# A one-token attention layer with a gated second branch: four 32 KB buffers become a ring of three

## The chip, the cores and the metric

The kernel runs on one core of one Trainium2 chip. The metric is the device time of one execution in microseconds. Before the change the median of five runs is 81.89 us (81.75 to 81.96).

## The reference

One token `x` (1 x 512) goes through two branches, and a scalar gate mixes them:

```python
g = sigmoid((x * gate_w).sum(-1))
q = (x @ wq).reshape(32 heads, 128)
k, v = k_cache[:, :, Sk - 4096:], v_cache[:, :, Sk - 4096:]   # 8 kv heads, 4 q heads on each
p = softmax(q @ k.T * 128 ** -0.5)
a = (p @ v).reshape(1, 4096) @ wo                             # wq: 512 x 4096, wo: 4096 x 512
b = (sigmoid(x @ w_gate) * (x @ w_up)) @ w_down               # 512 x 1792, 512 x 1792, 1792 x 512
out = g * a + (1 - g) * b
```

All tensors are bf16. `wq` and `wo` hold 4 MB each, the used part of `k_cache` and of `v_cache` 8 MB each, the three matrices of the second branch 1.75 MB each. All of it is read once.

## The kernel before

The kernel is written with tile pools: a tile is asked for with a tag, the tiles of a tag rotate through the `bufs` buffers of the pool, and a tile that takes over a buffer waits until the readers of the tile before it are done. The waits are put in by the framework from the order of the program.

Large loads are all issued from SP, whose queue is in order, so the program's order of loads is the order in which they are issued: `wq` (L76), K 0-3 and K 4-7 (L79, called from L85), `w_gate` (L89), `w_up` (L91), V 0-3 and V 4-5 (L79), V 6, the first half of `w_down` (L105), V 7, the second half of `w_down` (L107), and `wo` in six pieces of 8, 8, 8, 5, 2 and 1 rows of each partition (L112). A digit behind K or V is the number of a kv head. A load that waits for a buffer holds up every load behind it. ACT issues the two 1 KB rows `x` and `gate_w` at the start and half of the result at the end; SP issues the other half (L295).

Three pools hold these loads, given in bytes of one partition. `big` has one buffer of 32 KB: `wq_sb` first, then `wo_sb`. `blk` has two buffers of 32 KB: K 0-3 and K 4-7, then V 0-3 in the buffer of K 0-3 and V 4-7 in that of K 4-7. `w14` has three of 14 KB, one for each matrix of the second branch, so nothing waits there.

The work of the engines, in order of the program:

- `x` is turned into a column on PE (L133, `xT`), and DVE and ACT make the gate from it (L141 to L150).
- q (L155 to L164): for each of four blocks of 1024 columns, eight matmuls on PE with `xT` spread over all columns (L160, four slices `c` of `wq`, two halves each, `c` in the outer loop), then a copy by ACT (L162) and a transpose by DVE (L163). DVE then places q in `qbig` (L172).
- scores (L178 to L188): for each kv head DVE transposes K (L180, `kT`, from `kn`) and PE multiplies (L185, eight matmuls, all heads in `S_ps`). `kT` shares a ring of four 8 KB buffers with `q_sb` and `qtT`.
- softmax and the second branch up to `hT` (L191 to L240) on DVE, ACT and PE.
- V (L257 to L279): two batches of four kv heads on PE (L267), with part of the product with `w_down` between them (L248, called from L263 and L274).
- the end: the rows of `wo` are added to the accumulator `a_ps` in the order of the pieces (L248, called from L292); two copies (L294 on DVE, L296 on ACT) and two stores of 512 bytes end the kernel.

Of the kernel before, what the change touches and what calls it, by code (L numbers as in the profile page):

```python
# [12 lines left out]
BF16 = mybir.dt.bfloat16  # L13
# [4 lines left out]
def kernel(  # L18
# [16 lines left out]
    P = 128  # L35
# [8 lines left out]
    KB = W // P  # L44
# [11 lines left out]
    NJ_A = NJ // 2  # L56

    const = ctx.enter_context(tc.tile_pool(name="const", bufs=1))
    big = ctx.enter_context(tc.tile_pool(name="big", bufs=1))
    blk = ctx.enter_context(tc.tile_pool(name="blk", bufs=2))  # L60
    w14 = ctx.enter_context(tc.tile_pool(name="w14", bufs=3))
    ktp = ctx.enter_context(tc.tile_pool(name="ktp", bufs=4))
    work = ctx.enter_context(tc.tile_pool(name="work", bufs=1))
# [9 lines left out]
    dq = nc.sync  # L73
    wq_sb = big.tile([P, DC, HQ * DH], BF16, name="wq_sb", tag="big")
    wq_v = A_wq.rearrange("(p c) n -> p c n", c=DC)
    dq.dma_start(wq_sb[:], wq_v)  # L76

    def load_blocks(t, cache, g0, n, at=0):
        dq.dma_start(t[:, at:at + n, :, :],  # L79
                     cache[0, g0:g0 + n, SBASE:SBASE + W, :].rearrange("g (p kb) d -> p g kb d", kb=KB))  # L80

    kn = []
    for i in range(2):
        t = blk.tile([P, 4, KB, P], BF16, name="kn", tag="blk")
        load_blocks(t, A_k_cache, 4 * i, 4)  # L85
        kn += [t[:, j] for j in range(4)]

# [7 lines left out]

    vv = []
    for i in range(2):
        t = blk.tile([P, 4, KB, P], BF16, name="vv", tag="blk")
        vv += [t[:, j] for j in range(4)]
        if i == 0:  # L100
            load_blocks(t, A_v_cache, 0, 4)
        else:
            load_blocks(t, A_v_cache, 4, 2)
            load_blocks(t, A_v_cache, 6, 1, at=2)
            dq.dma_start(wd_sb[:, 0:NJ_A, :], wd_v[:, 0:NJ_A, :])  # L105
            load_blocks(t, A_v_cache, 7, 1, at=3)
            dq.dma_start(wd_sb[:, NJ_A:NJ, :], wd_v[:, NJ_A:NJ, :])  # L107
# [220 lines left out]
```

## Time and profile before

| what | value |
|---|---|
| median of five runs | 81.89 us (81.75 to 81.96) |
| the profiled execution, its own time | 81.75 us |
| its span, from the first to the last instruction | 80.0 us |
| busy: PE, DVE, ACT, POOL | 48.6, 35.1, 8.8, 5.0 us |
| bytes read, mean rate over the span | 30.67 MB, 384 GB/s |
| packet time of SP's queue, share of 16 DMA engines over the span | 92.4% |
| mean granted TensorE clock | 0.893 |

Busy time is the time in which an engine executes; a line of the chain of waits says what the work that ended last was waiting for, step by step from the end. A wait on SP (`SPq`) is a load that could not be issued. "DMA share" in a table by stage is packet time divided by 16 engines and the length of the stage; packets of one engine overlap a little, so it can be a few hundredths over 1. The span leaves out 1.75 us of the profiled execution's time, which lie around it.

### The profile page before, as it was taken

To read this page: it belongs to the slowest core of one execution; us is meant where nothing else is said; L and a number is where in the kernel's file an instruction comes from. 1 tells how busy PE (TensorE), PEld (TensorE's weight loads), DVE (VectorE), ACT (ScalarE), POOL (GpSimd) and SP (SyncE) were. 2 spreads that over 40 slices of the span, in tenths; PEclk is the share of its full clock that TensorE was granted. 3 is DMA by queue.
4 is the path that set the end of the run, shared out by engine and by line. 5 is a ranking of instruction groups with operands and counts; after the bars stand their busy time and mean duration, and the time that the engine had idled before them with its cause. 6 is when DMAs were issued, how large, how long until landed. Compare 5 with 4: busy or idle time off the path is not lost.

```text
span 80.0 us, 774 instructions
## 1 busy us (share of the span) xinstructions
PE 48.6 (61%) x313; PEld 22.8 (29%) x313; DVE 35.1 (44%) x43; ACT 8.8 (11%) x13; POOL 5.0 (6%) x10
## 2 busy tenths in 40 slices
PE   0010114999800099999998980006999699679560
PEld 0000111344200033344443430003333445356330
DVE  0000820014359999999995449998000000020020
ACT  2400000055630000000000036000000200200010
POOL 7970000000000000000000000000000000000000
PEclk9999999999999655699999999555558999999999
DMA  5879979999999999999999999999999999999500
GB/s 148 311 328 525 443 344 381 422 430 430 422 422 430 410 430 423 425 459 430 409 411 418 418 414 426 422 418 430 412 413 429 429 420 422 426 402 403 214 10 1
DMA packets 3738, 30.71 MB, mean 384 GB/s; under 512 B 276, under 2 KB 408, under 8 KB 920
## 3 DMA queue, kind: packets, MB, share of 16 engines
q1 hardware_dynamic: 3730, 30.67, 92.4%
q8 instruction: 2, 0.03, 0.2%
q10 hardware_dynamic: 6, 0.00, 0.0%
HBM read 30.67 MB, written 0.00 MB: 384 GB/s over the span
## 4 chain that ended last, share of the span: by engine, by line
DMA 56%; DVE 23%; PE 12%; issue 3%; ACT 1%; DVEq 0%
DMA wo_sb<-in_A_wo_dram 23%; DVE kT L180 20%; DMA vv<-in_A_v_cache_dram 18%; DMA wq_sb<-in_A_wq_dram 15%; PE q_ps L160 11%; DVE qbig L172 2%; PE a_ps L248 2%; ACT q_sb L162 1%; DVE qtT L163 1%; DVE res L294 1%; DVEq L180 0%; DVEq L172 0%
## 5 line engine op out<-in xcount | busy, mean ns | idle before, releaser
L185 PE MATMUL S_ps<-kT,qbig 128*128 128x512 bf16 x64 | 17.0, 428 | 6.4 <-DVE kT L180 6.4
L180 DVE STREAM_TRANSPOSE kT<-kn 128x2048 f32<-128x2048 f32 x8 | 17.7, 2274 | 0.0
L267 PE MATMUL pv_ps<-vv,eT 128*16 128x512 bf16 (+1 forms) x64 | 12.0, 464 | 0.0
L185 PEld LDWEIGHTS <-qbig 128*128 128x128 bf16 x64 | 6.8, 106 | 16.5 <-issue 6.6
L160 PE MATMUL q_ps<-wq_sb,xT 128*128 128x512 bf16 x32 | 8.6, 436 | 2.8 <-DMA wq_sb<-in_A_wq_dram 2.8
L163 DVE STREAM_TRANSPOSE qtT<-q_sb 128x512 f32<-128x512 f32 x4 | 2.8, 711 | 9.6 <-ACT q_sb L162 9.6
L279 DVE TENSOR_TENSOR oT<-o_ps,rb 128x16 bf16<-128x16 f32 x2 | 0.4, 176 | 14.5 <-PE o_ps L277 14.5
L267 PEld LDWEIGHTS <-eT 128*16 128x16 bf16 (+1 forms) x64 | 4.5, 103 | 6.4 <-issue 3.6
L160 PEld LDWEIGHTS <-xT 128*128 128x128 bf16 x32 | 3.5, 110 | 7.5 <-issue 4.9
L162 ACT CAST q_sb<-q_ps 128x1024 bf16<-128x1024 f32 x4 | 4.0, 1012 | 8.2 <-PE q_ps L160 8.2
L248 PE MATMUL a_ps<-wo_sb,oY 128*1 128x256 bf16 x64 | 4.2, 272 | 1.1 <-DMA wo_sb<-in_A_wo_dram 1.1
L237 PE MATMUL rb_ps<-lsel,ones_f 128*128 128x32 f32 x2 | 0.6, 397 | 6.9 <-DVE lsel L235 6.9
L141 DVE TENSOR_TENSOR gpr<-xr 1x512 f32<-1x512 bf16 x1 | 0.7, 680 | 8.2 <-DMA xr<-in_gate_w_dram 8.2
L126 POOL MEMSET qbig<- 128x4160 bf16 x1 | 3.6, 3566 | 0.0
L248 PEld LDWEIGHTS <-oY 128*1 128x1 bf16 x64 | 2.8, 83 | 2.4 <-issue 1.5
L133 PE MATMUL xt_ps<-ident,xr 1*128 1x1 bf16 x4 | 0.3, 165 | 5.2 <-POOL ident L118 5.2
L272 ACT COPY pv_sb<-pv_ps 128x512 f32<-128x512 f32 x2 | 1.2, 586 | 19.1 <-PE pv_ps L267 19.1
L221 ACT ACTIVATE sge<-gu_ps 128x448 f32<-128x448 f32 x1 | 0.5, 544 | 24.6 <-PE gu_ps L215 24.6
L144 PE MATMUL z_ps<-gsum,ones_f 1*128 1x1 f32 x2 | 0.6, 358 | 4.2 <-DVE gsum L142 4.2
L224 DVE RECIPROCAL sg<-sge 128x448 f32<-128x448 f32 x1 | 3.0, 2953 | 0.0
L277 PE MATMUL o_ps<-identf,pv_sb 128*128 128x16 f32 x16 | 2.1, 265 | 1.4 <-ACT pv_sb L272 1.4
L294 DVE CAST res<-a_ps 1x256 bf16<-1x256 f32 x1 | 0.4, 411 | 5.8 <-PE a_ps L248 5.8
(49 smaller groups left out, 28.2 us busy)
## 6 DMA issues: line engine op xcount, KB each, us to landing
kn<-in_A_k_cache_dram SPq DMA_DIRECT2D x2, 4096.0 KB
wq_sb<-in_A_wq_dram SPq DMA_DIRECT2D x1, 4096.0 KB, 12.3
vv<-in_A_v_cache_dram SPq DMA_DIRECT2D x1, 4096.0 KB, 18.2
wo_sb<-in_A_wo_dram SPq DMA_DIRECT2D x3, 1024.0 KB, 22.7
vv<-in_A_v_cache_dram SPq DMA_DIRECT2D x1, 2048.0 KB
vv<-in_A_v_cache_dram SPq DMA_DIRECT2D x2, 1024.0 KB, 16.5
wg_sb<-in_B_w_gate_dram SPq DMA_DIRECT2D x1, 1792.0 KB, 35.0
wu_sb<-in_B_w_up_dram SPq DMA_DIRECT2D x1, 1792.0 KB, 32.5
```

The costliest lines, as they stand in the source:

```text
L126: nc.gpsimd.memset(qbig[:], 0.0)
L160: nc.tensor.matmul(q_ps[:, hb, :], lhsT=xT[:, c:c + 1].to_broadcast([P, P]), rhs=wq_sb[:, c, n0:n0 + 512], start=(c == 0), stop=(c == DC - 1))
L162: nc.scalar.copy(q_sb[:, k * 1024:(k + 1) * 1024], q_ps[:].rearrange("p a b -> p (a b)"))
L163: nc.vector.transpose(qtT[:].bitcast(F32)[:, k * 512:(k + 1) * 512], q_sb[:].bitcast(F32)[:, k * 512:(k + 1) * 512])
L172: nc.vector.tensor_copy(q_dst[rows, :, 32 * qd:32 * qd + REP, :, t], q_src[rows, :, :, :, 0, t])
L180: nc.vector.transpose(kT[:].bitcast(F32), kn[g].rearrange("p k d -> p (k d)").bitcast(F32))
L185: nc.tensor.matmul(S_ps[:, hb, :], lhsT=q_st[:, g, dhi, :, t], rhs=k_v[:, hb * 16:(hb + 1) * 16, dhi, :, t], start=(g == 0 and dhi == 0 an ...
L224: nc.vector.reciprocal(sg[:], sge[:])
L248: nc.tensor.matmul(a_ps[32 * i:32 * i + 1, i, 0:HN], lhsT=lhsT, rhs=rhs[:, i * HN:(i + 1) * HN], start=start, stop=stop)
L267: nc.tensor.matmul(pv_ps[32 * gq:32 * gq + mm, :, :], lhsT=eT[:, g, 4 * m:4 * m + wj, :].rearrange("p k h -> p (k h)"), rhs=vv[g][:, 4 * m ...
L277: nc.tensor.matmul(o_ps[:], lhsT=pv_sb[:, j, :], rhs=sel_v[:, j, :, :], start=(j == 0), stop=(j == 3))
L294: nc.vector.tensor_copy(res[0:1, :], a_ps[0:1, 0, 0:HN])
```

## The change

The pool `blk` goes away. `wq`, K 0-3, K 4-7, V 0-3, V 4-7 and `wo` now share one ring of three 32 KB buffers under one tag. They take the buffers in this order, so V 0-3 follows `wq`, V 4-7 follows K 0-3, and `wo` follows K 4-7. The memory used for them is the same, three times 32 KB. The load of `wq` is cut in two: slices 0 and 1 of all 4096 columns, then slices 2 and 3, 2 MB each, with rows of 16 KB in place of 32 KB.

```diff
-    big = ctx.enter_context(tc.tile_pool(name="big", bufs=1))
-    blk = ctx.enter_context(tc.tile_pool(name="blk", bufs=2))
+    big = ctx.enter_context(tc.tile_pool(name="big", bufs=3))
...
-    dq.dma_start(wq_sb[:], wq_v)
+    for i in range(2):
+        dq.dma_start(wq_sb[:, 2 * i:2 * i + 2, :], wq_v[:, 2 * i:2 * i + 2, :])
...
-        t = blk.tile([P, 4, KB, P], BF16, name="kn", tag="blk")
+        t = big.tile([P, 4, KB, P], BF16, name="kn", tag="big")
...
-        t = blk.tile([P, 4, KB, P], BF16, name="vv", tag="blk")
+        t = big.tile([P, 4, KB, P], BF16, name="vv", tag="big")
```

The order of instructions on PE, DVE and POOL stays as it was, and on SP there is one load more, right behind the first. The waits of the loads become these: V 0-3 waits for the last matmul that reads `wq` (before: for the transpose of K 3); V 4-5 waits for the transpose of K 3 (before: of K 7); the first piece of `wo` waits for the transpose of K 7 (before: for the last matmul that reads `wq`). Each load also waits, as before, until the eighth load before it has landed, since eight semaphores go round among the loads; as there is one more load, this count is shifted by one.

## The prediction

> **What bounds the kernel now.** I read the 40 slices first, then the chain of waits in order of time, then a table by stage, then the waits of SP's queue and of PE.
>
> ```profile
> DMA  5879979999999999999999999999999999999500
> GB/s 148 311 328 525 443 344 381 422 430 430 422 422 430 410 430 423 425 459 430 409 411 418 418 414 426 422 418 430 412 413 429 429 420 422 426 402 403 214 10 1
> q1 hardware_dynamic: 3730, 30.67, 92.4%
> ```
>
> From the fourth slice to the thirty-seventh the 16 DMA engines are full but for one slice. Only the first three slices (6 us) and the end are thin.
>
> ```profile
> 0.74 12.32 DMA wq_sb<-in_A_wq_dram
> 13.10 8.61 PE q_ps L160 x32
> ...
> 25.43 7.54 DVE kT L180 x4
> ...
> 36.44 6.67 DVE kT L180 x3
> 43.10 0.02 issue
> 43.12 14.39 DMA vv<-in_A_v_cache_dram
> 57.51 0.02 issue
> 57.53 18.44 DMA wo_sb<-in_A_wo_dram
> 75.97 0.04 issue
> 76.01 1.27 PE a_ps L248 x16
> ```
>
> Read forward, the chain invites a wrong conclusion: `wq` lands, q is made, K is transposed, the buffer of K 4-7 comes free at 43.1 and only then is V 4-7 issued; so a buffer that comes free earlier would pull everything behind 43.1 forward. That holds only if the DMA engines had nothing to do while SP waited. The table by stage answers that:
>
> ```profile
> 24.00:28.00 4.00, 0.21 (x1) 0.20 (x2) 3.93 (x9) 0.00 (x0) 0.00 (x0) 0.81 1.01 422
> 32.00:36.00 4.00, 4.00 (x17) 1.68 (x16) 4.00 (x3) 0.00 (x0) 0.00 (x0) 0.84 1.03 438
> 40.00:44.00 4.00, 3.71 (x18) 1.56 (x16) 3.09 (x2) 0.00 (x0) 0.00 (x0) 1.00 0.98 411
> 48.00:52.00 4.00, 0.00 (x0) 0.00 (x0) 3.97 (x3) 1.20 (x2) 0.00 (x0) 0.80 1.01 422
> ```
>
> The last two columns are DMA share and GB/s. Around both waits of SP the share is 0.98 to 1.03. The records of landings say the same by load: 16 engines land K 0-3 at 22.4 to 22.95, K 4-7 at 32.4 to 32.9, `w_gate` at 36.7 to 37.2, `w_up` at 41.0 to 41.5, V 0-3 at 50.9 to 51.4 (one engine at 52.55). K 0-3 to K 4-7 took 9.95 us for 4 MB, and `w_up` to V 0-3 took 9.92 us for 4 MB. A hole ahead of V 0-3 would make its interval the longer one; there is none.
>
> ```profile
> SPq L79 <- DVE kT L180: 19.6, 2, 11.3
> SPq L112 <- DMA vv<-in_A_v_cache_dram: 11.8, 3, 5.0
> PE a_ps L248 <- DMA wo_sb<-in_A_wo_dram: 1.1, 2, 0.6
> ```
>
> SP does wait 19.6 us for transposes of K, and nobody pays: V 0-3 is issued at 34.35, when the queued loads last until 41.5 (7.1 us of cover); V 4-7 at 43.12, when V 0-3 lasts until 51.4 (8.3 us). At the end PE waits twice for `wo`, 0.57 and 0.54 us, so compute is about 1.1 us ahead of the stream in all. The kernel is 30.67 MB through a full stream, with 1.3 us of PE, 0.4 of a copy and the stores behind it.
>
> **The change, part by part.**
>
> V 0-3 behind `wq`: its wait now ends with the last matmul of L160, near 21 us instead of 34.3. V 4-5 moves from 43.1 to about 33.5. Both go behind loads that keep the engines full anyway: minus 0. SP's queue holds what stands behind V 0-3 (V 4-7, `w_down`, `wo`) and nothing that is due earlier; q's end is on no load's path except this one, and V 0-3 could be issued as late as 41 without a hole. If that cover were gone, each microsecond of lateness would cost one.
>
> `wo` behind K 4-7: the first piece was issued at 46.63; it now waits for the transpose of K 7, which ended at 43.1. Behind it the wait is the landing of earlier loads, as before: the third piece still waits for V 0-3, the fourth for V 4-5. `wo` is needed at 71.9, and at 43.1 the stream has work until 66.8 (landing of the second half of `w_down`): 0, with over 20 us of cover.
>
> `wq` in two loads, on SP: one more issue, 0.40 us and 0.06 between issues. K 0-3 goes out 0.46 us later, at 1.66 instead of 1.20; its first packet is not wanted before 12.12. Nothing. SP's issues are held back when many packets are outstanding (`w_gate` took 6.71 us to issue); eight more packets on each engine lengthen that, still long before 22 us.
>
> `wq` in two loads, on the DMA engines, which is on the path: each engine carried 8 rows of 32 KB at 1.213 us; it now carries 16 rows of 16 KB. The trace has no 16 KB row on this queue, so I bound it. From K's 8 KB rows (0.311 us): 4 x 0.311 - 1.213 = 0.031 us for three more packets, 0.010 each. Eight more packets: +0.08 us; a second completion packet of 4 bytes, 0.009: together +0.09. The rows of 14 KB (0.540) and 5 KB (0.200) lie on the same line (0.0105 us plus 0.0367 us for each 1000 bytes gives 0.537 and 0.198). A partial row at the pitch of 32 KB is what `wo` has in its 8 KB rows, and they take 0.311 as well, so reading half rows is not dearer. The other end: at the start the first packet of 13 engines took 1.68 to 2.27 us instead of 1.21, a mean excess of about 0.75. If half of that goes with half the packet: -0.37. If the second load pays such a start again: +0.75. I take +0.09, because at a boundary between two loads in the trace (`wq` to K) packets of the next load start at 12.12, when the first engines end their last row of `wq`: no restart there. And all 16 first packets end within 3.6 to 4.2 whether they began at 1.76 or 2.98, so the start looks like a fixed delay, not a slow rate.
>
> A rule speaks against cutting a load. The Trainium skill, page "DMA: Bandwidth & Descriptors", section "Anatomy of one DMA — SWDGE (gpsimd) path", gives each transfer a fixed cost of about 2.0 us beside its bytes, most of it completion, as a fit for loads issued by GpSimd. By it the sum would be 83.8 on the profiled time; the row at 12.12 above, for loads issued by SP, shows no such gap in the stream.
>
> q: the first half of `wq` lands near 8 (first rows end at 3.6 to 4.2, three more rows' worth is 3.6, the landing some 0.3 behind), so the four matmuls of slices 0 and 1 of the first block can run before 13.1. PE starts slow: of the 32 matmuls the first eight come every 0.38 to 0.43 us, the rest every 0.2155. Four fewer at the end of a run with the same slow stretch save 4 x 0.2155 = 0.86 us; four slow ones at most 1.7. K's transposes begin that much earlier (25.43 to about 24.6) and go through without a stop, since K 4-7 lands at 33.0 and the fifth transpose would come at 33.4. All compute behind moves 0.9 us forward, and PE waits longer for `wo`: 0 on the end.
>
> **Sum.** Profiled execution 81.75 + 0.09 = 81.84; it lies 0.14 below the median of the five, so the median becomes 81.89 + 0.09 = 81.98.
>
> **Rivals.**
>
> A. As above: 81.98; with the scatter of the phases of the 16 engines (0.5 us between first and last landing of one load) 81.75 to 82.25.
>
> B. Faster: the start is a rate and not a delay; half-size first packets end 0.37 earlier, less 0.09: 81.61. For: the thin first three slices (148, 311, 328 GB/s) are the only loose part of the stream. Against: the late starters' first packets, 1.2 to 1.3 us.
>
> C. Slower: the second load of `wq` makes each engine start anew, +0.75 + 0.09: 82.73. It decides as soon as the packets of the second load begin over 0.16 us behind the end of the first. Against: the boundary at 12.12.
>
> D. Slower by the end of the stream: two fetches of instructions, 16 KB each (packets of 1.06 us at 44.6 and 1.10 at 69.6), each hit one DMA engine in the trace, and that engine lands its share of all later loads 1.1 us after the others (52.55 against 51.44; 75.89 and 75.97 against 74.80 for the fourth piece of `wo`). They hit two engines. If both hit one, that one lands 1.1 later: 83.1. I see nothing in the change that selects the engine.
>
> E. Faster, more: V earlier does what the chain suggests, up to the 1.1 us that PE waits at the end: 80.8. Against it stands the share of 0.98 to 1.03 around both waits.
>
> **How the numbers follow.** A measurement of this kernel can tell about 0.2% (0.16 us) from no change. A 0.60, B 0.18, C 0.10, D 0.07, E 0.05. Of A's 0.60, 0.40 lies within 0.16 us, 0.18 above (its centre is 0.09 up), 0.02 below. Faster: 0.02 + 0.18 + 0.05 = 0.25; same 0.40; slower: 0.18 + 0.10 + 0.07 = 0.35. The range reaches from B's time with a little of the phases, 81.45, to C's 82.75; outside lie D, most of E and the rims of B and C.
>
> **What would show it.** In the profile after: SP's wait for `kT` at L79 falls from 19.6 us, and DMA share stays about 1 with landings of K 0-3 within 0.3 us of 22.95: then V's earlier issue is worth nothing. Intervals of 9.9 us between landings of 4 MB stay. q's matmuls show four before 13 us and end near 20.9. PE waits longer than 1.1 us for `wo`. B is shown by K 0-3 landing before 22.7, C by landing after 23.5, D by one engine landing 2.2 us after the rest, and I am wrong altogether if the stream after 25 us runs at another rate than 420 to 430 GB/s.

## Result and profile after

The changed kernel takes 82.20 us (median of 46 executions, 81.73 to 82.76) against 81.91 us before (86 executions, 81.64 to 82.26): ratio 1.0036, 95% interval 1.0024 to 1.0047, so slower by about 0.3 us. The range held the time; the centre, 81.98, was 0.2 us too low. In a ratio, executions more than 1.5% above the fastest of their kernel are left out as slow; here that drops two, the 82.72 and 82.81 of the merged loads on the kernel before.

Two things said ahead of the prediction need setting right. The 32 KB buffers are three before and three after (one in `big`, two in `blk`, then one ring), not four as in the title. And the order of instructions on PE did not stay as it was: in the trace of the changed kernel the first block of q ends with the twelfth matmul instead of the eighth, because the framework put the first halves of two blocks in front.

The medians hide the shape. The executions of the kernel before form one group. Those of the changed kernel form two: 24 between 81.73 and 82.25 with a median of 81.9, which is the time of before, and 22 between 82.38 and 82.76 with a median of 82.54. Nearly half of the executions pay about 0.64 us, the others nothing. The profiled execution (81.91 us, span 80.1) is of the first group, so it shows the change without what it costs.

The page of the changed kernel, slices of the span: full as before, a little later at the start.

```profile
DMA  3899999999999999999999999999999999999500
GB/s 74 303 410 417 458 434 380 434 421 434 413 425 421 421 421 435 441 437 422 422 400 417 417 421 425 425 417 417 423 418 423 422 422 433 397 430 395 194 12 1
q1 hardware_dynamic: 3874, 30.67, 92.3%
```

Its chain of waits in order of time:

```profile
1.17 11.80 DMA wq_sb<-in_A_wq_dram
12.98 0.04 issue
13.02 7.49 PE q_ps L160 x24
...
24.22 8.90 DVE kT L180 x4
33.12 0.02 issue
33.14 24.64 DMA vv<-in_A_v_cache_dram
57.78 0.02 issue
57.80 18.36 DMA wo_sb<-in_A_wo_dram
76.16 0.04 issue
76.20 1.28 PE a_ps L248 x16
```

V 4-5 is issued 10 us earlier than before (33.1 for 43.1) and lands no earlier (57.8 for 57.5): the issue has moved, the stream has not. q ends at 20.5 instead of 21.7, and K's transposes begin at 24.22 instead of 25.43. The waits of SP and of PE:

```profile
SPq L79 <- DVE kT L180: 10.2, 1, 10.2
SPq L79 <- PE q_ps L160: 7.5, 1, 7.5
PE a_ps L248 <- DMA wo_sb<-in_A_wo_dram: 2.8, 3, 1.5
```

The last line is the one that matters: PE now waits 2.8 us for `wo` in three gaps, where it waited 1.1 in two. Compute is further ahead of the stream, and the end of PE's timeline in this execution looks so (start, length, instructions, idle time before them):

```profile
70.24 1.04 PE L248 MATMUL a_ps<-wo_sb,oY 128*1 128x256 bf16 x16
72.13 1.04 PE L248 MATMUL a_ps<-wo_sb,oY 128*1 128x256 bf16 x16 [0.84 <-DMA wo_sb<-in_A_wo_dram]
74.64 1.04 PE L248 MATMUL a_ps<-wo_sb,oY 128*1 128x256 bf16 x16 [1.48 <-DMA wo_sb<-in_A_wo_dram]
76.20 1.24 PE L248 MATMUL a_ps<-wo_sb,oY 128*1 128x256 bf16 x16 [0.53 <-DMA wo_sb<-in_A_wo_dram]
```

### The profile page after: what moved, and what is told of

It is laid out like the page before. It is cut to its first block, busy times and chain, and to the rows that moved or that the text cites. A ratio compares the mean times of both kernels' runs of the same rounds, so it can differ in the third digit from the quotient of the medians.

```text
span 80.1 us, 776 instructions
## 1 busy us (share of the span) xinstructions
PE 50.4 (63%) x313; PEld 23.1 (29%) x313; DVE 35.1 (44%) x43; ACT 8.9 (11%) x13; POOL 5.0 (6%) x10
## 4 chain that ended last, share of the span: by engine, by line
DMA 68%; DVE 15%; PE 11%; ACT 1%; issue 1%; SPq 0%; DVEq 0%
DMA vv<-in_A_v_cache_dram 31%; DMA wo_sb<-in_A_wo_dram 23%; DMA wq_sb<-in_A_wq_dram 15%; DVE kT L180 11%; PE q_ps L160 9%; DVE qbig L172 2%; PE a_ps L248 2%; ACT q_sb L162 1%; DVE qtT L163 1%; DVE res L294 0%; SPq L76 0%; DVEq L172 0%
## 5 line engine op out<-in xcount | busy, mean ns | idle before, releaser
L160 PE MATMUL q_ps<-wq_sb,xT 128*128 128x512 bf16 x32 | 11.1, 521 | 0.8 <-DMA wq_sb<-in_A_wq_dram 0.8
L267 PE MATMUL pv_ps<-vv,eT 128*16 128x512 bf16 (+1 forms) x64 | 11.5, 445 | 0.0
L221 ACT ACTIVATE sge<-gu_ps 128x448 f32<-128x448 f32 x1 | 0.5, 544 | 24.6 <-PE gu_ps L215 24.6
L272 ACT COPY pv_sb<-pv_ps 128x512 f32<-128x512 f32 x2 | 1.2, 586 | 18.6 <-PE pv_ps L267 18.6
L277 PEld LDWEIGHTS o_ps<-identf,pv_sb 128*128 128x128 f32 x16 | 1.9, 191 | 2.4 <-ACT pv_sb L272 2.4
## 6 DMA issues: line engine op xcount, KB each, us to landing
vv<-in_A_v_cache_dram SPq DMA_DIRECT2D x1, 2048.0 KB, 24.6
```

The source lines that it names most:

```text
L160: nc.tensor.matmul(q_ps[:, hb, :], lhsT=xT[:, c:c + 1].to_broadcast([P, P]), rhs=wq_sb[:, c, n0:n0 + 512], start=(c == 0), stop=(c == DC - 1))
L267: nc.tensor.matmul(pv_ps[32 * gq:32 * gq + mm, :, :], lhsT=eT[:, g, 4 * m:4 * m + wj, :].rearrange("p k h -> p (k h)"), rhs=vv[g][:, 4 * m ...
L272: nc.scalar.copy(pv_sb[:], pv_ps[:])
L277: nc.tensor.matmul(o_ps[:], lhsT=pv_sb[:, j, :], rhs=sel_v[:, j, :, :], start=(j == 0), stop=(j == 3))
```

## Experiments

Three explanations of the second group were set against each other, in each of which it comes with the early q or with the two loads of `wq` (S: start of the DMA engines; C: a halved clock of PE at the end; F: the instruction fetches), and a fourth in which it comes with V's early issue (V).

**The two halves of the change, one at a time.** The ring alone keeps `wq` in one load:

```diff
-    for i in range(2):
-        dq.dma_start(wq_sb[:, 2 * i:2 * i + 2, :], wq_v[:, 2 * i:2 * i + 2, :])
+    dq.dma_start(wq_sb[:], wq_v)
```

> The ring of three with wq in one load. The changed kernel runs 0.36% over the kernel before, and its executions fall into two groups, near 81.9 us and near 82.55 us. Theory S (start): the rows of 16 KB spread the 16 DMA engines differently at the start. Theory C (cold tail): q is ready about 1.2 us earlier, PE waits longer for wo, and its clock is halved before the last 16 matmuls (1.28 us become up to 2.5). Theory F (fetch): the earlier compute moves the two instruction fetches, and they delay a DMA engine more in some executions. All three expect no second group here, since q starts at 13.1 us as before: ratio 1.000, all executions 81.65 to 82.25. A theory V (V's early issue itself disturbs the stream) expects 1.003 to 1.004 with the second group.

Measured: 0.9995 (0.9975 to 1.0015), 12 executions from 81.64 to 82.14. No second group, so V's early issue gains or costs nothing beyond 0.2%, and V falls. The split alone keeps the two old pools:

```diff
-    dq.dma_start(wq_sb[:], wq_v)
+    for i in range(2):
+        dq.dma_start(wq_sb[:, 2 * i:2 * i + 2, :], wq_v[:, 2 * i:2 * i + 2, :])
```

> The two old pools with wq in two loads, so q starts early but V keeps its late issue. Theories S, C and F expect the second group near 82.55 and a ratio of 1.003 to 1.004. Theory V expects 1.001 (the 0.09 us of the eight more packets per engine) and one group.

Measured: 1.0023 (0.9997 to 1.0049); nine executions up to 82.2 and three at 82.34, 82.44 and 82.65. The ratio alone doesn't settle it, and the kernel before, run beside it, reaches 82.36. But the three long ones have a mean granted clock of 0.865 to 0.868, lower than any of the 35 executions of before (0.873 to 0.929), which points to the split and to the clock.

**The changed kernel once more**, for a profile of the other group:

> The changed kernel again, unaltered, for the share of the slower group on the same chip and for a profile that may fall in it. Ratio 1.0036 (1.002 to 1.005). If the profile is of the slower group: theory C expects the last 16 matmuls at a clock of 0.5 and the last piece of wo landing at the usual 76.2 to 77.1; theory F expects one DMA engine landing wo about 0.6 us later than in the other group, at a clock of 1.0 at the end; theory S expects K 0-3 landing 0.6 us late.

Measured: 1.0025 (0.9993 to 1.0056); six executions up to 81.88, one at 82.20, five from 82.45 to 82.75, and the profile fell on the longest. PE at the end of it:

```profile
72.31 1.04 PE L248 MATMUL a_ps<-wo_sb,oY 128*1 128x256 bf16 x16 [0.59 <-DMA wo_sb<-in_A_wo_dram]
74.82 1.04 PE L248 MATMUL a_ps<-wo_sb,oY 128*1 128x256 bf16 x16 [1.47 <-DMA wo_sb<-in_A_wo_dram]
76.39 1.87 PE L248 MATMUL a_ps<-wo_sb,oY 128*1 128x256 bf16 x16 [0.53 <-DMA wo_sb<-in_A_wo_dram]
```

The last 16 matmuls take 1.87 us in place of 1.24. The table by stage of the same execution (the last three numbers of a row: granted clock, DMA share, GB/s) shows the clock behind it:

```profile
72.00:74.00 2.00, 1.04 (x16) 0.69 (x16) 0.00 (x0) 0.00 (x0) 0.00 (x0) 1.00 0.98 398
74.00:76.20 2.20, 1.04 (x16) 0.69 (x16) 0.00 (x0) 0.00 (x0) 0.00 (x0) 1.00 0.50 186
76.20:78.40 2.20, 1.87 (x16) 0.88 (x15) 0.11 (x1) 0.07 (x1) 0.00 (x0) 0.52 0.03 10
```

From 76.3 on the granted clock is 0.5; PE has 1.04 us of work in each of the two stages ahead of it. In the profile of the first group the same stage runs at 1.00:

```profile
76.20:78.40 2.20, 1.24 (x16) 0.68 (x15) 0.41 (x1) 0.36 (x1) 0.00 (x0) 1.00 0.02 8
```

The two spans differ by 0.82 us: 0.63 are these 16 matmuls, 0.19 a later landing of `wo` (they begin at 76.39 for 76.20). The late landing is that of the DMA engine hit by the first instruction fetch: V 0-3 lands on it 1.7 us after the others here, 1.45 in the first group's profile. The ring alone has 1.6 there, its `wo` lands as late (76.3), and it has no second group; so the fetches spread the times within a group and do not make the second one. K 0-3 has landed by 22.98, as before, so S has nothing to point to.

This is the only profiled execution of the second group. Of the 22 above, five have a mean granted clock of 0.866 to 0.869, like this one (0.866); the other 17 have 0.894 or 0.895, a value that occurs in the first group too. That the last matmuls of these 17 are lengthened in the same way is inferred, not seen.

**The early q taken back, the rest kept:**

```diff
-        for c in range(DC):
+        for c in (2, 3, 0, 1):
...
-    ... start=(c == 0), stop=(c == DC - 1))
+    ... start=(c == 2), stop=(c == 1))
```

> The changed kernel with the slices of wq taken in the order 2, 3, 0, 1, so that the first matmul of q waits for the second load: both loads and the ring stay, the early start of q goes. Theory S expects the second group to stay, 1.003 to 1.004. Theories C and F expect it to go: one group, 1.001 (0.09 us of packets). Theory V expects it to stay.

Measured: 1.0001 (0.9983 to 1.0018), 12 executions from 81.70 to 82.15. With both loads of `wq` and the ring, but q no longer early, the second group is gone. S falls: the cost comes with the early q. The clock (C) and the fetches (F) are left.

**PE kept busy between the pieces of `wo`:**

```diff
+    warm = ps_big.tile([P, 2, 512], F32, name="warm", tag="b")
     for c in range(NC_O):
         add_row(oY[:, c:c + 1], wo_sb[:, c, :], False, c == NC_O - 1)
+        for i in range({15: 5, 23: 2}.get(c, 0)):
+            nc.tensor.matmul(warm[0:32, i % 2, :], lhsT=oY[:], rhs=wo_sb[:, c, :], start=True, stop=True)
```

> The changed kernel with seven more matmuls (128x512, into a spare PSUM tile that nothing reads) in the idle time of PE between pieces of wo: five behind row 15, two behind row 23, 0.216 us each. q stays early, the loads stay. Theory C (cold tail): the clock stays at 1.0 to the end, the slower group near 82.5 goes, ratio 1.000 to 1.0015. Theory F (the instruction fetches come earlier with the earlier compute): the slower group stays, ratio 1.0025 to 1.004.

Measured: 0.999 (0.9972 to 1.0009), 12 executions from 81.75 to 82.17. PE does more, and the second group is gone, while q is as early as in the changed kernel and the second fetch (68.2 us) lies where it lay there (67.8 and 68.4 in the two profiles). F falls. One reserve: this ran on another chip than the repeat above, beside the kernel before but without the unaltered changed kernel; if half of the executions were still long, twelve short ones would be a chance of about 1 in 2500. PE's timeline and the last stage:

```profile
73.05 1.24 PE L295 MATMUL warm<-wo_sb,oY 128*32 128x512 bf16 x5
74.67 1.04 PE L248 MATMUL a_ps<-wo_sb,oY 128*1 128x256 bf16 x16 [0.38 <-DMA wo_sb<-in_A_wo_dram]
75.54 0.59 PE L295 MATMUL warm<-wo_sb,oY 128*32 128x512 bf16 x2
76.25 1.22 PE L248 MATMUL a_ps<-wo_sb,oY 128*1 128x256 bf16 x16
```

```profile
76.20:78.40 2.20, 1.22 (x16) 0.68 (x15) 0.41 (x1) 0.36 (x1) 0.00 (x0) 1.00 0.03 9
```

**Early compute without the change.** The kernel before, with one transpose of K left out:

```diff
-        kT = ktp.tile([P, KB * P], BF16, name="kT", tag="kt")
-        nc.vector.transpose(kT[:].bitcast(F32), ...)
+        if g != 5:
+            kT = ktp.tile([P, KB * P], BF16, name="kT", tag="kt")
+            nc.vector.transpose(kT[:].bitcast(F32), ...)
```

> The kernel before with one part left out: the transpose of K for kv head 5 (its scores are made from the transposed K of head 4). Compute is then 2.2 us earlier from the scores on, with the loads of before. Theory C: PE has 1.04 us of work in each 2.5 us of the end, its clock is halved before the last 16 matmuls in most executions, and a kernel that does less is slower: most executions 0.6 to 1.2 us over the kernel before, ratio 1.004 to 1.012. A plain reading of the stream as the bound expects 1.000; theory F expects 1.000 to 1.004 with some executions near 82.5.

Measured: 1.005 (1.0026 to 1.0074), but not for the expected reason alone. In its profile compute is 1.1 us earlier than before at the end (`oY_ps` at 70.01 for 71.08), not 2.2. The profiled execution has the halved clock at the end, behind the same kind of gaps:

```profile
74.34 1.04 PE L249 MATMUL a_ps<-wo_sb,oY 128*1 128x256 bf16 x16 [1.47 <-DMA wo_sb<-in_A_wo_dram]
75.94 1.87 PE L249 MATMUL a_ps<-wo_sb,oY 128*1 128x256 bf16 x16 [0.56 <-DMA wo_sb<-in_A_wo_dram]
```

Yet only three of its 12 executions have a span of 80.5 us or more; nine have 79.9 to 80.2, like the kernel before, where most were expected to be long. And its time lies 2.2 us over its span where that of before lies 1.8 over it, which no part of the span explains. So one profile shows the halved clock with earlier compute and no change of loads; the ratio is not a measure of that, and how often it happens was guessed too high.

**A version that beats both.** Since the stream is the bound, fewer packets should pay:

```diff
-    WO_SPLIT = (0, 8, 16, 24, 29, 31, 32)
+    WO_SPLIT = (0, 16, 24, 29, 31, 32)
...
-            load_blocks(t, A_v_cache, 4, 2)
-            load_blocks(t, A_v_cache, 6, 1, at=2)
-            dq.dma_start(wd_sb[:, 0:NJ_A, :], wd_v[:, 0:NJ_A, :])
-            load_blocks(t, A_v_cache, 7, 1, at=3)
-            dq.dma_start(wd_sb[:, NJ_A:NJ, :], wd_v[:, NJ_A:NJ, :])
+            load_blocks(t, A_v_cache, 4, 4)
+            dq.dma_start(wd_sb[:], wd_v)
```

On the kernel before:

> The kernel before with fewer and longer packets: V 4-7 in one load, w_down in one load behind it (rows of 14 KB in place of two of 7 KB), wo in pieces of 16, 8, 5, 2 and 1 rows. By the price of 0.0105 us for each packet and 0.009 for each completion: 16 packets and 4 completions fewer on each engine, -0.20 us, ratio 0.9975, if the end hangs on the stream alone and the later landing of V 7 (66.8 in place of 64.7) still finds PE occupied. If packets cost nothing: 1.000. PE is busier between pieces of wo (32 matmuls for the first piece), so theory C expects no slower group.

Measured: 0.9967 (0.9937 to 0.9997), 12 executions spread from 81.44 to 82.81. The median of all twelve is 81.79, against 82.00 of before. The best ones are 0.2 us under the best of before, as expected, and in the profiles the 14 DMA engines that no fetch delayed land the last row of `wo` at 75.06 to 75.64 instead of 75.25 to 75.77. The long ones were not expected: the five longest have a mean granted clock of 0.872 to 0.874, the other seven 0.910 to 0.929. The profiled execution took 82.81. Its clock is halved in the middle of the end, from 71.7 to 75.2; in the stage ahead PE was busy for 2.2 of 3.4 us, about half of it in small matmuls (L274, 128x16):

```profile
68.30:71.70 3.40, 2.21 (x18) 1.31 (x17) 0.44 (x3) 0.59 (x1) 0.00 (x0) 1.00 1.00 419
71.70:75.20 3.50, 3.50 (x38) 2.19 (x36) 0.14 (x1) 0.00 (x0) 0.00 (x0) 0.51 0.89 350
```

PE's timeline shows the price:

```profile
71.54 2.99 PE L245 MATMUL a_ps<-wd_sb,hT 128*1 128x256 bf16 x28
74.32 4.08 PE L245 MATMUL a_ps<-wo_sb,oY 128*1 128x256 bf16 x64
```

The 28 matmuls with `w_down`, all of them now behind V, take 2.99 us, and in the next kernel, at the full clock, 1.69. Here compute is late: the last piece of `wo` has landed by 76.9, and PE ends at 78.4. On the changed kernel, where compute has 1.2 us more:

> The changed kernel with the same merged loads. Theory C: the first piece of wo now brings 32 matmuls (2.1 us) at 72.3, PE is busy for most of the window ahead of the last piece, so the slower group goes; with +0.09 for the two loads of wq and -0.20 for the merged ones: 0.9985. Theory F expects the slower group to stay: 1.001 to 1.002.

Measured: 0.9966 (0.9949 to 0.9984), 12 executions from 81.57 to 81.87, one tight group with the lowest median of this round. The gain is larger than the 0.9985 expected, and what makes the rest of it was not looked for. PE is busy in long pieces and not late:

```profile
69.72 1.69 PE L245 MATMUL a_ps<-wd_sb,hT 128*1 128x256 bf16 x28
72.03 1.91 PE L245 MATMUL a_ps<-wo_sb,oY 128*1 128x256 bf16 x32 [0.61 <-DMA wo_sb<-in_A_wo_dram]
74.51 1.04 PE L245 MATMUL a_ps<-wo_sb,oY 128*1 128x256 bf16 x16 [0.57 <-DMA wo_sb<-in_A_wo_dram]
76.10 1.22 PE L245 MATMUL a_ps<-wo_sb,oY 128*1 128x256 bf16 x16 [0.56 <-DMA wo_sb<-in_A_wo_dram]
```

## Why the prediction was right or wrong

**The bound: right.** The stream was full and stays so; loads land where they landed: V 0-3 at 50.9 to 51.4 with one engine at 52.8 (before: 52.55).

**V and `wo` in other buffers, minus 0: right,** and shown alone by the ring (0.9995). The chain's "V at 43.1" was an issue, not a landing; rival E, which read it as the bound, is out. SP's wait for `kT` fell from 19.6 to 10.2 as foretold and bought nothing.

**Packets of `wq`, +0.09: too large, and its sign is not shown.** Averaged over the 16 engines, K 0-3 lands at 22.66 to 22.72 in the four profiles with `wq` in one load (mean 22.68) and at 22.62 to 22.74 in the six with two (mean 22.70): +0.02, well within their scatter. The row price itself holds (a 16 KB row took 0.611 us; the line gave 0.612). What may have offset it is the start: in the profiles of the two kernels the first 16 KB packets took 0.6 to 1.5 us and the first 32 KB ones 1.2 to 2.3, so a part of rival B's gain may have been there. How the two split was not measured by itself. Rivals C and D did not occur: K 0-3 had landed by 22.92, not after 23.5, so the second load paid no restart, and the two fetches still hit two engines.

**q earlier by 0.86: right in kind, too small.** Eight matmuls of the first half of `wq` ran in front, not four; K's transposes began 1.21 us earlier. That is one pair of profiles: over all of them they begin at 22.9 to 24.6 with the early q and at 25.4 to 26.5 without, depending on when PE's granted clock comes up (11.4 to 18.6 us).

**"PE waits longer for `wo`: 0 on the end": the step that failed.** The wait itself costs nothing, but PE, waiting in gaps of 0.6 to 1.5 us, was granted half the clock, and the 16 matmuls of the last pieces of `wo` are the part of PE's work that nothing hides. In the profile of the second group they take 1.87 us at the lower clock instead of 1.24, which is 0.63. The 22 of 46 executions of that group are 0.64 longer: 0.48 x 0.64 = 0.31 us, about the whole of the measured 0.29. The term was missing from the sum, and no rival held it. That the time lay inside the range was luck to this extent: "slower" came out of the packets in the text, and out of the clock on the chip.

The Trainium skill, page "TensorE: Matmul & The Clock Gate", has the pieces: its Part 1 says that the clock is set by activity in a free-running window of about 3.4 us, which agrees with these traces, where the time between two changes of the granted clock runs from 3.41 to 20.48 us and is always a whole multiple of 3.413 (20.48 is six of them). The changes also fall at other moments in each execution (58.33 and 78.81 in the first group's profile of the changed kernel, 59.22 and 76.28 in the second's). That this shift is why the same program falls into two groups is an inference. Its section "Why this matters for your kernels" asks only for no idle gap above some 3 us. Here the measurement differs: the longest gap ahead of the halved clock is 1.47 us. The first row is the second group's profile, in the 3.41 us before the change at 76.28; the second row is the first group's, in the 3.41 us before 75.40, which lies one such length ahead of its change at 78.81:

```profile
72.87:76.28 3.41, 1.52 (x26) 0.94 (x21) 0.00 (x0) 0.00 (x0) 0.00 (x0) 1.00 0.66 256
71.98:75.40 3.42, 1.80 (x31) 1.30 (x31) 0.00 (x0) 0.00 (x0) 0.00 (x0) 1.00 0.88 349
```

With PE busy for 1.52 us, or 45%, the clock was halved; with 1.80 us, 53%, it stayed. Taken in the same way, the run without one transpose had 41% and was halved, and the split alone had 49% and stayed. But in the merged kernel on the old pools a stage with 2.21 of 3.40 us, 65%, was followed by the halved clock, so the busy share of the profile is not by itself what decides; the exact condition stays open.

## What to carry to other kernels

When a stream bounds the kernel, ask for each wait of SP how much is still queued, and let an earlier issue count only if the queue would have run dry. Then look at what runs behind the last landing: it is the one compute that is never hidden, and making the compute ahead of it earlier can make it slower, if the engine then idles in short gaps and its clock drops. Merge pieces so that the engine works in long stretches up to the last landing, and look at all executions, not at the median: two groups 0.64 us apart were the clue that no profile of the first group could give.

## What was not expected of the hardware

Short gaps can be enough to halve the clock: 0.59 and 1.47 us of waiting between bursts of 1.04 us came ahead of it in one execution. Gaps of 0.84 and 1.48 us did not bring it in time in another, so the moment counts too.

A small load can wait long beside large rows of another queue's load: the 1 KB row `gate_w`, issued by ACT at 1.3 us, landed at 7.6 to 8.3 in the four profiles with 32 KB rows of `wq` and at 6.5 to 6.7 in the six with 16 KB rows.

One 16 KB instruction fetch comes with a delay of 1.0 to 1.7 us on one DMA engine for the rest of the stream; there are two fetches in each profiled execution, on two engines, and all loads behind land with these engines. Where the second fetch moved (69.6 before, 73.3 and 71.4 with merged loads), the second late engine moved with it. The kernel's last 1.1 us of streaming is theirs (before, the last row of `wo` lands by 75.77 on 14 engines and at 76.84 and 76.92 on these), and no experiment here tried to remove them.
